# A ScalarE copy of a transposed bf16 tile, with its operands named as fp32

## The chip, the core and the metric

One core of a Trainium2 chip runs one launch of a hand-scheduled kernel. The metric is the device time of a launch in microseconds (us). The core has five engines that run their own instruction streams in order and meet at semaphores: TensorE (PE in the profile; its weight loads are PEld), VectorE (DVE), ScalarE (ACT), GpSimd (POOL) and SyncE (SP), which issues most DMAs.

## What is computed

A transformer block in which attention and a SwiGLU feed-forward stand side by side, forward and backward. Sequence S = 2048, width D = 448, 16 heads of 28, hidden width F = 1792, all operands bf16:

```python
def _fwd_reference(A_x, A_wqkv, A_wo, B_x, B_w_gate, B_w_up, B_w_down):
    x = A_x
    xn = _layernorm(x, axis=-1)
    return x + _A_ref(xn, A_wqkv, A_wo) + _B_ref(xn, B_w_gate, B_w_up, B_w_down)
...
    _out, _vjp = jax.vjp(_f, A_x, A_wqkv, A_wo, B_w_gate, B_w_up, B_w_down)
    _grads = _vjp(grad_out)
```

`_A_ref` is softmax attention over 16 heads, `_B_ref` is (silu(x w_gate) * (x w_up)) w_down. The outputs are the block's output and the gradients of x, wqkv, wo, w_gate, w_up and w_down.

## The kernel before

The launch has three stages. Up to about 626 us the forward attention runs (64 slots of four heads for each of four groups of heads), with the feed-forward and the weight gradients as fillers on TensorE. From there to about 1393 us the attention's backward pass runs; this is the stage the change touches. The rest is the tail, which ends the gradient of x.

The backward stage walks 512 steps (`steps`, L807): group g of four heads, pair of heads hp, key chunk kc of 512, query chunk qc of 512, query tile qi of 128. Four steps, one of each qi, are a block, so there are 128 blocks. At step k the main loop (L1337) issues:

- `row(k)` (L826): four TensorE matmuls of 32x128 by 32x512 in four row groups of the array: two scores of step k into `sb` tiles (L834), two products dP of step k - 1 into `db` tiles (L842).
- `ew(k)` (L854): two ScalarE exps, 128x512 fp32 in PSUM to bf16 `e_sb` (L858), and two VectorE products of step k - 1, `db` times `e_sb` into bf16 `ds_sb` (L864). For the query tiles 0, 1 and 2 of a block, SyncE then issues a DMA that transposes `ds_sb` into `dsT` (L851).
- `kv(k')` (L926): the matmuls that add a step's part of dk and dv into the one `acc` tile (L937, L941). After the last step of a key chunk, every 16 steps, ScalarE copies `acc` into `dkv` (L947).
- where k % 4 is 0, `tr_unit(b)` (L914): the fourth ds tile of block b (in the last block the third too) is not transposed by DMA but by TensorE: eight 128x128 transposes (L919) into one bf16 PSUM tile of 128x1024 that is taken from the `db` tiles, and ScalarE copies it into `dsT` (L924). In the last block the third tile's copy is VectorE's (L922).
- where k % 4 is 1, `dq_unit(b)` (L958): sixteen matmuls of the transposed ds against k (L968) into a `genb` tile, which ScalarE scales into `dq_acc` or `dq_st` (L972, L981); GpSimd then adds `dq_st` to `dq_acc` (L983, L985). In the last group VectorE takes the last of these (L977).
- between these, fillers (`fill_open`, `fill_step`, L1233 to L1251) that use TensorE for other work and one `genb` tile at a time: late weight gradients (`late_dw`, L903), the block's output y (`y_unit`, L1093, evacuated by VectorE at L1098 or L1101), the feed-forward's part of dx (`dx_unit`, L1149; for the first third of F, `fq == 0`, ScalarE evacuates it at L1155, later VectorE adds it at L1157), the attention's part (`dc_unit`, L1196, VectorE at L1200), transposes of dk, dv and dq (`dsp_unit`, `dsq_unit`, L1021, L1002, VectorE at L1024, L1005) and the gradient of wqkv (`dwq_unit`, L1034, VectorE at L1041 to L1044).

The order on every engine is that of these calls: the kernel is recorded with a manual schedule (L132). PSUM is shared out by pools: three `sb` tiles, three `db` tiles (which the transposes share with `row`), one `acc` and one `genb`. A matmul into a tile waits until the tile's last reader is done: for `sb` an exp, for `db` a VectorE product or the copy of L924, for `genb` its evacuation.

The tile that the copy reads and the part of `dsT` that it writes are both 128 partitions of 1024 bf16 elements that lie next to each other, 2048 bytes a partition.

Of the kernel before, what the change touches and what calls it, by code (L numbers as in the profile page):

```python
# [11 lines left out]
FP32 = mybir.dt.float32  # L12
# [93 lines left out]
def kernel(  # L106
# [23 lines left out]
    PE, DVE, ACTE, POOL, SP = nc.tensor, nc.vector, nc.scalar, nc.gpsimd, nc.sync  # L130
# [539 lines left out]
    for t in range(4):  # L670
        run(T_unit(xnT, xn_t, t, t % 2 == 0, ps_s if t < 2 else None))
    DVE.tensor_reduce(out=r_ones[:],
                      in_=ident_f[:].rearrange("p (a b) -> p a b", b=HP)[:, :, 28:30],
# [240 lines left out]
    def tr_unit(b):  # L914
        for qi in (3,) if b < NB // 4 - 1 else (2, 3):
            ds = dss.pop(4 * b + qi)
            ps = ps_b.tile([P, 8, P], BF16, name="db", bufs=3)
            for c in range(8):
                PE.transpose(ps[:, c, :], ds[:, c // 4, (c % 4) * P:(c % 4 + 1) * P], ident_bf[:])  # L919
            o = dsT[b][:, qi].rearrange("p j kt s -> p (j kt) s")  # L920
            if qi == 2:
                DVE.tensor_copy(out=o, in_=ps[:])  # L922
            else:
                ACTE.copy(out=o, in_=ps[:])  # L924

    def kv(k):  # L926
        g, hp, kc, qc, qi = steps[k]
# [409 lines left out]
    for k in range(NB + 12):  # L1337
# [21 lines left out]
        if m == 0:  # L1359
            b = (k - 8) // 4  # L1360
            if 9 <= k < NB and cur is None:
                fill_open(600)
            fill_step(R0)
            if 0 <= b < NB // 4:
                tr_unit(b)
            fill_step(BIG)
        elif m == 1:
            b = (k - 13) // 4
            if 0 <= b < NB // 4:
                dq_unit(b)  # L1370
            if k > NB and k < NB + 8:
                while stream:
                    for _ in stream.pop(0)[1]():
                        pass
                if k < NB + 4:
                    dx_mm(0)
                else:
                    dx_a(0)
                    dx_mm(2)
        elif m == 2:  # L1380
            if 9 <= k < NB:
                fill_open(BIG)
                fill_step(R2)
        else:
            fill_step(R3)
# [59 lines left out]
```

## Time and profile before

| | |
|---|---|
| median of 3 runs | 1437.01 us (1435.54 to 1440.87) |
| span of the profiled execution | 1438.2 us |
| mean granted TensorE clock | 0.982 of full speed |
| ScalarE busy | 1264.2 us of the span |
| of it exps of the backward stage (L858) | 1024 x 611 ns, 555.0 us |
| of it the copy of L924 | 128 x 1016 ns, 130.0 us |
| of it dq evacuations (L981, L972) | 120, 48.0 us |
| of it dkv (L947) | 32 x 709 ns, 22.7 us |
| of it dxg (L1155) | 16 x 560 ns, 9.0 us |
| VectorE products (L864) | 1024 x 685 ns, 646.5 us |

The profile is one execution. Busy times of operations that overlap in an engine's pipeline are counted once, so a group's busy time is less than its count times the mean of one. An idle time before an instruction is named with what ended it: `[0.20 <-PE db L842]` is 0.20 us of idle that ended when TensorE's instruction of L842, into `db`, was done. TensorE's matmuls are pipelined and their ends are modelled: the start of one against the start of the next says more than the busy share. The granted clock is the share of TensorE's full clock that was allowed.

Busy tenths of the span in 40 slices of 36 us, TensorE, VectorE and ScalarE:

```
PE   5899999989999999989999989999999999999995
DVE  6677757656666676578999989888899999999988
ACT  4799988989889998869999989999989999899974
```

### The profile page before, as it was taken

The numbers are of one execution on the slowest core, as the hardware profiler recorded it, in microseconds if no ns is written. First come the engines' busy times: TensorE is split into PE (matmuls) and PEld (weight loads), VectorE is DVE, ScalarE is ACT, GpSimd is POOL, SyncE is SP. The second block draws the span as 40 slices with busy tenths as digits, with TensorE's granted clock in tenths as the row PEclk, the third lists the DMA queues.
The fourth block names the chain that finished last, engine by engine and source line by source line (L and its number), as shares of the span: only waits on it lengthen the run. The fifth ranks groups of instructions, "written<-read, shape, count | busy, mean of one in ns | idle before, by whom it ended". The sixth has DMA issues, their size and how long they took to land. (4 is left out here: it accounts for less than half of the span.)

```text
span 1438.2 us, 34638 instructions
## 1 busy us (share of the span) xinstructions
PE 1321.2 (92%) x12625; PEld 539.0 (37%) x12686; DVE 1154.8 (80%) x2001; ACT 1264.2 (88%) x2190; POOL 411.8 (29%) x577
## 2 busy tenths in 40 slices
PE   5899999989999999989999989999999999999995
PEld 2333333333333333333343434433443334443333
DVE  6677757656666676578999989888899999999988
ACT  4799988989889998869999989999989999899974
POOL 6574514454434454211121211201111112020005
PEclk9999999999999999989999999999999999999998
DMA  5796957796578676699999999999999999999981
GB/s 154 183 205 160 237 116 169 179 190 157 149 164 191 153 155 153 176 243 233 219 213 227 206 227 173 221 219 223 223 169 200 200 216 218 212 186 207 190 142 60
DMA packets 681116, 270.22 MB, mean 188 GB/s; under 512 B 607338, under 2 KB 655970, under 8 KB 680946
## 3 DMA queue, kind: packets, MB, share of 16 engines
q1 hardware_dynamic: 672498, 254.78, 87.1%
q0 software_dynamic: 7040, 12.93, 4.1%
q8 instruction: 99, 1.62, 0.5%
q14 instruction: 71, 0.58, 0.1%
q10 hardware_dynamic: 1408, 0.30, 0.1%
HBM read 64.37 MB, written 59.62 MB: 86 GB/s over the span
## 5 line engine op out<-in xcount | busy, mean ns | idle before, releaser
L864 DVE TENSOR_TENSOR ds_sb<-db,e_sb 128x512 bf16<-128x512 f32 x1024 | 646.5, 685 | 48.6 <-issue 22.4
L858 ACT ACTIVATE e_sb<-sb 128x512 bf16<-128x512 f32 x1024 | 555.0, 611 | 53.7 <-PE db L842 37.1
L628 ACT ACTIVATE eT<-s_w 128x1024 bf16<-128x1024 f32 x256 | 263.8, 1030 | 47.0 <-PE s_ps L625 43.8
L630 ACT ACTIVATE eT<-s_ps 128x512 bf16<-128x512 f32 x512 | 280.2, 611 | 0.0
L842 PE MATMUL db<-kd,qd 32*128 32x512 bf16 x1024 | 238.0, 385 | 8.6 <-DVE ds_sb L864 7.5
L834 PE MATMUL sb<-kd,qd 32*128 32x512 bf16 x1024 | 210.9, 389 | 5.3 <-DMA qd<-QD_d 3.4
L983 POOL TENSOR_TENSOR dq_acc<-dq_acc,dq_st 128x256 f32<-128x256 f32 x64 | 46.4, 724 | 497.7 <-ACT dq_st L981 497.7
L941 PE MATMUL acc<-ds_sb,qd 128*32 128x512 bf16 x1024 | 161.3, 391 | 0.0
L937 PE MATMUL acc<-e_sb,qd 128*32 128x512 bf16 x1024 | 159.2, 392 | 1.3 <-DVE dw_o L544 1.3
L924 ACT COPY dsT<-db 128x1024 bf16<-128x1024 bf16 x128 | 130.0, 1016 | 18.4 <-PE db L919 17.3
L396 POOL TENSOR_TENSOR nn<-nn,ag 128x512 f32<-128x512 f32 x56 | 71.3, 1274 | 249.7 <-DVE ag L394 241.1
L625 PE MATMUL s_ps<-QQ,KK 32*128 32x512 bf16 x512 | 126.2, 385 | 4.1
L1149 PE MATMUL genb<-wguT,dau_c 128*128 128x448 bf16 x448 | 117.5, 355 | 6.3 <-ACT dq_st L981 3.9
L625 PE MATMUL s_w<-QQ,KK 32*128 32x512 bf16 x512 | 100.2, 387 | 12.8 <-ACT eT L628 9.8
L834 PEld LDWEIGHTS <-qd 32*128 32x128 bf16 x1024 | 48.2, 91 | 146.3 <-issue 136.9
L437 PE MATMUL gen<-xn_t,f_sp 128*128 128x448 bf16 x416 | 91.8, 354 | 2.6 <-DVE nn L411 1.7
L437 PEld LDWEIGHTS <-f_sp 128*128 128x128 bf16 x640 | 55.7, 98 | 76.7 <-issue 31.6
L919 PE MATMUL db<-ident_bf,ds_sb 128*128 128x128 bf16 x1032 | 80.3, 222 | 0.9 <-DVE ds_sb L864 0.9
L968 PE MATMUL genb<-dsT,kd 128*32 128x256 bf16 x2048 | 79.2, 274 | 1.1
L919 PEld LDWEIGHTS <-ds_sb 128*128 128x128 bf16 x1032 | 69.1, 99 | 23.6 <-issue 5.1
L397 POOL TENSOR_TENSOR nn<-nn,tt 128x512 f32<-128x512 f32 x56 | 72.1, 1287 | 4.4
L625 PEld LDWEIGHTS <-KK 32*128 32x128 bf16 x1024 | 29.1, 91 | 115.3 <-issue 112.5
(179 smaller groups left out, 1951.7 us busy)
## 6 DMA issues: line engine op xcount, KB each, us to landing
F_d<-hda SPq DMA_DIRECT2D x56, 384.0 KB
dau_c<-F_d SPq DMA_DIRECT2D x24, 512.0 KB
qd<-QD_d SPq DMA_DIRECT2D x16, 512.0 KB
kd<-KD_d SPq DMA_DIRECT2D x16, 384.0 KB
dsT<-ds_sb SPq DMA_TRANSPOSE x383
h_c<-F_d SPq DMA_DIRECT2D x8, 512.0 KB
wT_d<-wT_f SPq DMA_DIRECT2D x14, 256.0 KB
KD_d<-qk_sp SPq DMA_DIRECT2D x7, 512.0 KB
```

The lines of the kernel that those rows point to most:

```text
L437: PE.matmul(ps[:, :D], lhsT=fsp[fc][:, t // 4, w, t % 4, :], rhs=rhs[:, t, :], start=(t == 0), stop=(t == NT - 1))
L625: PE.matmul(sp4[hh], lhsT=KK[g][r:r + HP, kt * P:(kt + 1) * P], rhs=QQ[g][r:r + HP, qsl], start=True, stop=True, tile_position=(r, 0))
L628: ACTE.activation(out=e2[0][:], in_=wide[:], func=ACT.Exp, scale=SCALE)
L630: ACTE.activation(out=e2[1][:, j], in_=sp4[2 + j], func=ACT.Exp, scale=SCALE)
L834: PE.matmul(s_ps[:], lhsT=qside[g, qc][r:r + HP, 0, qi * P:(qi + 1) * P], rhs=kside[g, kc][r:r + HP, 0, :], start=True, stop=True, tile_po ...
L842: PE.matmul(d_ps[:], lhsT=qside[g, qc][r:r + HP, 1, qi * P:(qi + 1) * P], rhs=kside[g, kc][r:r + HP, 1, :], start=True, stop=True, tile_po ...
L858: ACTE.activation(out=est[k][:, j], in_=sps.pop((k, j))[:], func=ACT.Exp, scale=SCALE)
L864: DVE.tensor_tensor(out=ds[:, j], in0=dps.pop((k - 1, j))[:], in1=est[k - 1][:, j], op=ALU.mult)
L919: PE.transpose(ps[:, c, :], ds[:, c // 4, (c % 4) * P:(c % 4 + 1) * P], ident_bf[:])
L924: ACTE.copy(out=o, in_=ps[:])
L937: PE.matmul(a[r:r + HP, :], lhsT=sp4[:, 1, r:r + HP], rhs=e[:, j, :], start=first, stop=last, tile_position=(0, r), skip_group_check=True)
L941: PE.matmul(a[r:r + HP, :], lhsT=sp4[:, 0, r:r + HP], rhs=ds[:, j, :], start=first, stop=last, tile_position=(0, r), skip_group_check=True)
```

## The change

```diff
@@ -921,7 +921,7 @@
             if qi == 2:
                 DVE.tensor_copy(out=o, in_=ps[:])
             else:
-                ACTE.copy(out=o, in_=ps[:])
+                ACTE.copy(out=o.bitcast(FP32), in_=ps[:].bitcast(FP32))
```

ScalarE's copy reads the same 2048 bytes of a partition and writes the same 2048 bytes, but both operands are named as 512 fp32 elements where they were 1024 bf16 elements. Two neighbouring bf16 values travel as the two halves of one fp32 word. Nothing else in the program's text changes: the transposes still write bf16, and the dq product still reads bf16. VectorE's one copy at L922 stays as it was.

## The prediction

> **What bounds the kernel now.** I read the page first for the engines and the costliest groups, then the busy time of single blocks (a block is the stretch from one L924 copy to the next, 128 in all), then the timelines of three kinds of block.
>
> ```profile
> PE 1321.2 (92%) x12625; PEld 539.0 (37%) x12686; DVE 1154.8 (80%) x2001; ACT 1264.2 (88%) x2190; POOL 411.8 (29%) x577
> L858 ACT ACTIVATE e_sb<-sb 128x512 bf16<-128x512 f32 x1024 | 555.0, 611 | 53.7 <-PE db L842 37.1
> L924 ACT COPY dsT<-db 128x1024 bf16<-128x1024 bf16 x128 | 130.0, 1016 | 18.4 <-PE db L919 17.3
> ```
>
> The copy is 130.0 us of ScalarE, all after 633 us. Now the busy times (length, PE, PEld, DVE, ACT, POOL) of an ordinary block, one that ends a dkv, one that evacuates dxg on ScalarE, and the whole steady stage:
>
> ```profile
> 1137.24:1142.87 5.63, 5.58 (x65) 2.18 (x64) 5.47 (x10) 5.35 (x11) 0.00 (x0) 1.00 1.16 153
> 1130.93:1137.24 6.31, 5.75 (x65) 2.36 (x64) 5.59 (x10) 5.79 (x12) 0.00 (x0) 1.00 1.01 193
> 948.53:954.44 5.91, 5.82 (x68) 2.37 (x67) 5.04 (x9) 5.71 (x13) 0.00 (x0) 1.00 1.07 236
> 660.00:1390.00 730.00, 695.33 (x7993) 292.26 (x7992) 669.48 (x1122) 673.74 (x1252) 107.34 (x165) 0.99 1.10 206
> ```
>
> In the ordinary block VectorE idles 0.16 us and ScalarE 0.28; in the dxg block ScalarE idles 0.20 and VectorE 0.87. So the engine with least slack changes from block to block, and each kind must be costed alone. An ordinary block (from 1095.95) on VectorE, ScalarE and TensorE:
>
> ```profile
> 1096.84 1.28 DVE L864 TENSOR_TENSOR ds_sb<-db,e_sb 128x512 bf16<-128x512 f32 x2
> 1098.28 3.74 DVE L864 TENSOR_TENSOR ds_sb<-db,e_sb 128x512 bf16<-128x512 f32 x6 [0.16 <-issue]
> ...
> 1100.61 1.09 ACT L858 ACTIVATE e_sb<-sb 128x512 bf16<-128x512 f32 x2 [0.20 <-PE db L842]
> ...
> 1096.02 0.80 PE L842 MATMUL db<-kd,qd 32*128 32x512 bf16 x2
> 1097.19 0.61 PE L968 MATMUL genb<-dsT,kd 128*32 128x256 bf16 x16
> 1097.74 0.39 PE L842 MATMUL db<-kd,qd 32*128 32x512 bf16 x2
> ```
>
> Its loop has no ScalarE in it. L842's 0.80 us is two matmuls of 0.37 to 0.39 with a stall between: the second waits for a db tile that VectorE frees at about 0.45 us into the block. From there TensorE issues without a gap (acc, the dq product, the next row at 1097.74), the row ends at 1098.13, VectorE starts at 1098.28 and runs six products, 3.74 us, whose end frees the db tile of the next block. 0.45 to 2.33 us on TensorE and 3.74 us on VectorE make 5.62 of 5.63. ScalarE waits 0.20 us for TensorE inside that time: it is not late.
>
> **The change, part by part.**
>
> *The price of one copy.* No row shows a 128x512 f32 to f32 copy from PSUM. Nearest are L1155, 128x448 f32 from f32, 560 ns, and the bf16 copies of 512 and 1024 elements (L340 587, L924 1016). The bf16 pair gives (1016-587)/512 = 0.838 ns an element; 560 + 64 x 0.838 = 614. Bounds: 587 (the bf16 copy of 512) and 640 (L386, 512 f32 to f32). I take 614, since L1155 has both operand types. Each copy ends 402 ns earlier (376 to 429), and the next ScalarE operation, which now starts 0.89 us after the copy starts, may start at 0.49. Over 128 copies ScalarE loses 51.5 us of work. What reaches the end is counted by kind of block:
>
> *Ordinary blocks and those that evacuate y (L1101):* nothing. The exp after the copy comes 0.40 earlier or, in the y blocks, still waits for a row that TensorE is late with (it starts 1.04 to 1.07 after the copy began, the copy having ended at 1.02); the next row is set by the loop above. The cover is ScalarE's own wait, which grows from 0.28 to 0.68. The same holds for the blocks of dwq (exp at 1.17 or later). If the cover were gone, 0.40 each would show.
>
> *The 16 blocks with L1155* (925 to 1025 us). There the dxg evacuation sits behind the copy, and TensorE's dq product, which reuses the genb tile, waits for it:
>
> ```profile
> 949.42 0.56 ACT L1155 COPY dxg<-genb 128x448 f32<-128x448 f32 x1
> 949.55 0.38 PE L937 MATMUL acc<-e_sb,qd 128*32 128x512 bf16 x2
> 950.03 0.62 PE L968 MATMUL genb<-dsT,kd 128*32 128x256 bf16 x16
> ```
>
> From that L937 to L968 are 0.48 us; in the ordinary block it is 0.21 (1096.98 to 1097.19). The evacuation can begin 0.33 earlier (genb's last matmul ends 0.51 into the block), so the whole stall goes: 0.26. What is late next is VectorE's loop of the ordinary block, at 5.63 to 5.65, just where 5.91 - 0.26 lands. 12 plain blocks x 0.26 = 3.1. In the four that also end a dkv (6.75 long, 8.07 once) ScalarE's chain copy, dxg, two exps, dkv, dq holds TensorE, which waits for dq; it moves by 0.33: 4 x 0.33 = 1.3.
>
> *Blocks that end a dkv.* ScalarE runs without a gap from the copy to the dq evacuation, and TensorE waits for it:
>
> ```profile
> 1132.79 0.72 ACT L947 ACTIVATE dkv<-acc,cols 128x512 bf16<-128x512 f32 x1
> 1132.17 0.38 PE L941 MATMUL acc<-ds_sb,qd 128*32 128x512 bf16 x2
> 1133.84 0.35 PE L1149 MATMUL genb<-wguT,dau_c 128*128 128x448 bf16 x1 [0.52 <-ACT dq_acc L972]
> ```
>
> dkv can't start before acc is done, 1132.55 to 1132.56, plus 0.06 to signal (so much later dkv starts in the one block where it waits for acc alone, at 840.18): 0.18 earlier than 1132.79, not 0.40. VectorE follows, having 0.37 and 0.26 us of waits in that block. Eleven blocks are of this form: 11 x 0.18 = 2.0. Two early ones and one before a dsp transpose give 0.45 together. In the other 14 of the 32 dkv blocks the exp is held by TensorE, or VectorE has no slack: nothing.
>
> *Six blocks after a dsp unit* (5.41 us, as 1114.27 to 1119.68) run on ScalarE and VectorE both; VectorE's wait of 0.12 goes: 0.7.
>
> *What the change adds.* As built, all engines keep their order, but the db tiles go round otherwise in four of the first eight blocks: the second db matmul of the row after the transposes gets the very tile that the copy frees, and waits for ScalarE where it waited for VectorE. Behind it on TensorE stand the acc matmuls, dq and the next row, for which VectorE waits. The copy lets go 0.66 after its start; that matmul starts 0.55 after it in three of the blocks and 0.18 in the first. Loss: 3 x 0.11 + 0.48 = 0.8; bounds 0 (a later wait covers it) and 1.5 (it comes again). The tail gains nothing: its last copies stand beside VectorE's dx work.
>
> Sum: 3.1 + 1.3 + 2.0 + 0.45 + 0.7 - 0.8 = 6.8 us, against the profiled execution's span of 1438.2, which is 1.2 above the median of the runs. Taken off the median: 1430.2. The price of the copy hardly matters: at 640 ns it still gives 376 ns, more than any block uses.
>
> The stage's occupancy is 673.74 us for ScalarE, 669.48 for VectorE. [...]
>
> **The rivals.**
>
> *VectorE takes over as the bound, and its waits go too.* If ScalarE's earlier exps also dissolved VectorE's 0.16 us in 36 ordinary blocks and 0.30 in 11 y blocks, 5.8 + 3.3 us would come on top: 1421.1. For it: VectorE is within 5 us of ScalarE over the stage. Against: the releaser of those waits is TensorE's row, which waits for VectorE.
>
> *Nothing arrives.* The blocks that gain are given back at the transposes by DMA or at the next dkv, or the copy in fp32 is no shorter: 1437. For it: three waits of VectorE for a ds tile that its DMA still reads, 3.1 us together. Against: 560 ns for 448 fp32 elements.
>
> *Slower: TensorE's clock drops more often.* Blocks with dsp transposes come with and without a drop: 7.80 us at a mean granted clock of 0.87 (716.17) against 7.04 at 1.00 (811.95), and 7.64 against 6.88. One drop costs 0.76. A shift of all phases can move drops; it decides from nine more on (6.8/0.76). With 20 more: 1437 - 6.8 + 15.2 = 1445. Against: the stage shows four or so in 730 us, and TensorE's idle time shrinks. [...]
>
> **How the numbers follow.** The forecast has 0.60, VectorE's bound 0.18, nothing 0.14, slower 0.08. About 0.5%, 7.2 us, is what a measurement can tell from no change: faster means below 1429.8. The forecast's own range is 1426 to 1434 (6.8 with a few drops or DMA waits either way, and the bounds above) and lies astride that line, about half on each side: 0.30 + 0.18 = 0.48 faster; 0.30 + 0.14 = 0.44 same; 0.08 slower. The range takes in the VectorE case and the case of nothing: 1420 to 1437.
>
> **What would show it.** L924 at about 614 ns x128, the ordinary block still at 5.63 with ScalarE idle about 0.68 in it, the dxg block at 5.65, the dkv block at 6.13, and L968 no longer held by L1155. An ordinary block below 5.55, or L924 above 700 ns, would make the prediction wrong; so would dxg blocks that stay at 5.91.

## The result, and the profile after

The changed kernel took 1433.64 us (median of 10 runs, 1429.33 to 1436.28), the kernel before 1440.36 us on the same chip (10 runs, 1435.54 to 1443.47). The ratio is 0.9962, 95% interval 0.9946 to 0.9977: 0.2% to 0.5% faster. The profiled execution of the changed kernel has a span of 1427.5 us, against 1438.2. Of those 10.7 us, 4.7 lie before the first L924 copy (at 628.5 us, before at 633.2), in a part that the change doesn't touch; from the first copy to the last it is 763.3 us before and 756.7 after, 6.6 us less; the tail is 0.7 longer.

Page of the changed kernel, first its engines, then two of the costliest groups (busy us, mean ns, idle time before):

```profile
PE 1318.6 (92%) x12625; PEld 540.2 (38%) x12686; DVE 1152.4 (81%) x2001; ACT 1219.0 (85%) x2190; POOL 411.0 (29%) x577
L858 ACT ACTIVATE e_sb<-sb 128x512 bf16<-128x512 f32 x1024 | 552.5, 601 | 75.8 <-PE db L842 58.0
L924 ACT COPY dsT<-db 128x512 f32<-128x512 f32 x128 | 75.4, 589 | 17.5 <-PE db L919 16.4
```

The copy does what the change says: 1016 ns have become 589. ScalarE lost 54.6 us of copying (130.0 less 75.4); the stage became 6.6 us shorter, an eighth of that. Part of the rest stands in the second line: before its exps ScalarE now waits 75.8 us, 22 more than before, mostly for TensorE. Before the dq evacuations (L981, L972) it waits 15 us more. And its whole busy time fell by 45.2 us only (1264.2 to 1219.0), as its operations overlap less: their single times add to 1473 us before and 1404 after, so that some 209 us overlapped before and 185 after.

The same kinds of block as in the prediction, now in the changed kernel (stretch, length; busy time of TensorE, weight loads, VectorE, ScalarE, GpSimd; clock, DMA share, GB/s). In this order: dxg on ScalarE, dxg with a dkv, after a dsp unit, a dkv, ordinary:

```profile
944.29:949.92 5.63, 5.63 (x68) 2.42 (x67) 5.04 (x9) 5.38 (x13) 0.00 (x0) 1.00 1.11 236
955.55:961.91 6.36, 5.79 (x68) 2.50 (x67) 5.15 (x9) 5.84 (x13) 0.73 (x1) 1.00 1.14 252
1106.08:1111.38 5.30, 5.30 (x65) 2.22 (x64) 5.25 (x10) 5.00 (x11) 0.73 (x1) 1.00 1.21 151
1122.64:1128.81 6.17, 5.83 (x65) 2.36 (x64) 5.49 (x10) 5.46 (x12) 0.00 (x0) 1.00 1.09 223
1128.81:1134.44 5.63, 5.58 (x65) 2.18 (x64) 5.47 (x10) 5.03 (x11) 0.00 (x0) 1.00 1.16 166
```

The ordinary block is 5.63 us as before; ScalarE's idle time in it grew from 0.28 to 0.60 and nothing else moved. The dxg block fell from 5.91 to the same 5.63, with TensorE now busy from end to end; with a dkv it fell from 6.75 to 6.36, the dkv block from 6.31 to 6.17, the block after a dsp unit from 5.41 to 5.30.

The dxg block of the changed kernel, from its timeline (start us, us, engine):

```profile
944.83 0.53 ACT L1155 COPY dxg<-genb 128x448 f32<-128x448 f32 x1
945.31 0.38 PE L937 MATMUL acc<-e_sb,qd 128*32 128x512 bf16 x2
945.53 0.61 PE L968 MATMUL genb<-dsT,kd 128*32 128x256 bf16 x16
```

From L937 to L968 are now 0.22 us, where 0.48 were. The evacuation starts 0.54 us into the block, not 0.89, and L968 has stopped waiting for it.

### The profile page after: what moved, and what is told of

It reads as the page before. It is cut to its first block, busy times and chain, and to the rows that moved or that the text cites. A ratio compares the mean times of both kernels' runs of the same rounds, so it can differ in the third digit from the quotient of the medians.

```text
span 1427.5 us, 34631 instructions
## 1 busy us (share of the span) xinstructions
PE 1318.6 (92%) x12625; PEld 540.2 (38%) x12686; DVE 1152.4 (81%) x2001; ACT 1219.0 (85%) x2190; POOL 411.0 (29%) x577
## 5 line engine op out<-in xcount | busy, mean ns | idle before, releaser
L858 ACT ACTIVATE e_sb<-sb 128x512 bf16<-128x512 f32 x1024 | 552.5, 601 | 75.8 <-PE db L842 58.0
L937 PE MATMUL acc<-e_sb,qd 128*32 128x512 bf16 x1024 | 158.3, 390 | 1.3 <-DVE dw_o L544 1.3
L625 PE MATMUL s_w<-QQ,KK 32*128 32x512 bf16 x512 | 100.0, 386 | 13.2 <-ACT eT L628 10.4
L924 ACT COPY dsT<-db 128x512 f32<-128x512 f32 x128 | 75.4, 589 | 17.5 <-PE db L919 16.4
L968 PE MATMUL genb<-dsT,kd 128*32 128x256 bf16 x2048 | 80.0, 277 | 0.0
```

What stands on the lines that cost most here:

```text
L625: PE.matmul(sp4[hh], lhsT=KK[g][r:r + HP, kt * P:(kt + 1) * P], rhs=QQ[g][r:r + HP, qsl], start=True, stop=True, tile_position=(r, 0))
L858: ACTE.activation(out=est[k][:, j], in_=sps.pop((k, j))[:], func=ACT.Exp, scale=SCALE)
L937: PE.matmul(a[r:r + HP, :], lhsT=sp4[:, 1, r:r + HP], rhs=e[:, j, :], start=first, stop=last, tile_position=(0, r), skip_group_check=True)
```

## The experiments

All kernels were profiled, and those compared in time ran 6 or 12 times, with the kernel before beside them on the same chip. Single runs of one kernel spread over 10 us and more, and go with the TensorE clock that they were granted: over 175 runs, with one straight line for all and a constant for each kernel on each chip, a clock lower by 0.01 goes with 9.4 us more, and 2.2 us of scatter remain, where 3.4 are left without the clock. Where "at equal clock" is said, it is the difference to the kernel before from that fit, with its 95% bounds; what a change does to the clock itself is not in it. Block lengths need none of this: undisturbed, one block of one kernel repeats from run to run to 0.01 us, seldom 0.02.

**The same kernel again, and the copy split by blocks.** Four kernels on one chip:

> The changed kernel a second time. Theory (the gain sits in blocks where ScalarE's copy stands before something that TensorE waits for): the same 5 to 7 us below the kernel before, and the same lengths of single blocks to 0.02 us (ordinary 5.63, dxg 5.63, dkv 6.17). Rival (the gain is a lucky placing of clock drops and DMA waits): the block lengths stay as they are, but the time moves by several us, as other blocks carry the drops.

> The copy named fp32 only in the 17 blocks from 48 to 64, where L1155 evacuates dxg on ScalarE; bf16 in the other 111. Theory: 12 x 0.28 + 4 x 0.38 = 4.9 us less than before, about 1435.5 where the kernel before has 1440.4, and dkv blocks elsewhere at 6.31. Rival (every copy pays its share): 17/128 of the gain, 0.8 us.

> The complement: bf16 in blocks 48 to 64, fp32 in the other 111. Theory: dxg blocks stay at 5.91 and 6.75; 11 dkv blocks x 0.135 + 6 blocks after a dsp unit x 0.12 + 0.4 = 2.6 us less than before, less up to 0.8 for the first eight blocks: 1.8 to 2.6. Rival (every copy pays its share): 111/128 of the gain, 5 to 6 us.

> fp32 from block 8 on; the first eight keep bf16 copies, and with them, if the tiles go round as before, the waits of the second db matmul for VectorE. Theory: at or up to 0.8 us below the changed kernel, and in blocks 5 to 7 the second db matmul starts some 0.55 after the copy, not 0.64. Rival (the early waits are hidden): the same time as the changed kernel.

```diff
+            elif 48 <= b < 65:
+                ACTE.copy(out=o.bitcast(FP32), in_=ps[:].bitcast(FP32))
             else:
                 ACTE.copy(out=o, in_=ps[:])
```

(the second, against the kernel before; the third has `not 48 <= b < 65`, the fourth `b >= 8`.) Measured, with the kernel before at 1438.62 (35 runs); lengths of blocks 52 (dxg), 82 (dkv) and 83 (ordinary):

| copy in fp32 | median, us | ratio, 95% | at equal clock, us | dxg | dkv | ordinary |
|---|---|---|---|---|---|---|
| everywhere, again | 1436.57 | 0.9985 (0.9962 to 1.0008) | -5.2 ± 1.5 | 5.63 | 6.18 | 5.63 |
| blocks 48 to 64 | 1436.70 | 0.9998 (0.9974 to 1.0022) | -3.0 ± 1.5 | 5.63 | 6.31 | 5.63 |
| all but 48 to 64 | 1439.54 | 1.0004 (0.9987 to 1.0022) | -1.3 ± 1.5 | 5.91 | 6.18 | 5.63 |
| from block 8 on | 1433.80 | 0.9968 (0.9947 to 0.9989) | -5.7 ± 1.4 | 5.63 | 6.18 | 5.63 |

The dxg block in the busy times of the second kernel:

```profile
949.46:955.09 5.63, 5.63 (x68) 2.41 (x67) 5.03 (x9) 5.38 (x12) 0.00 (x0) 1.00 1.09 218
```

and in those of the third:

```profile
950.26:956.17 5.91, 5.82 (x68) 2.37 (x67) 5.03 (x9) 5.71 (x12) 0.00 (x0) 1.00 1.09 224
```

Lengths follow the naming block by block, to 0.01 us. Seventeen copies of 128 carry 3.0 us of gain and the other 111 1.3, which add to 4.3 of the 5.2. The 3.0 ± 1.5 falls short of the 4.9 that were expected and that the lengths of these blocks show; why, the record doesn't tell. The rival by which each copy pays its share, 0.8 and 5 to 6, is out. The medians alone would not have told this: at 12 runs each their intervals hold no change in three of the four. The rival of lucky drops is out for the block lengths, but by the fit drops are what makes the median of the repeat so much nearer to that of the kernel before. Its mean clock was 0.9773 beside 0.9799; in the runs of the first result it was 0.9799. All four kernels here had a lower clock than the kernel before (0.9773 to 0.9790); the kernels with moved evacuations below had a slightly higher one (0.9798 to 0.9803 beside 0.9790 and 0.9791). Whether the change brings some more drops stays open.

The early wait is there and of the predicted size: in blocks 5 to 7 the second db matmul starts 0.64 us after the copy in the changed kernel and 0.55 in the fourth one, 0.09 each. In the time it can't be seen. The first block took between 6.28 and 10.28 us over these and the next profiles, half-clock stretches (a granted clock of 0.50 from 632 to 636 us in the kernel before) and loads that come late included.

**What of the copy pays: its time on ScalarE, or that it lets go sooner?**

> The fp32 copy, with a second ScalarE copy of 288 bf16 elements from SBUF to a scratch tile behind it, some 0.4 us: ScalarE has about the time of the kernel before, but frees the db tile and finishes dsT early. Theory (what pays is that the operations behind the copy come earlier): all of the gain goes, dxg blocks back at 5.9, dkv blocks at 6.31, ordinary at 5.63. Rival (what pays is the early release of db or dsT): dxg 5.63 and dkv 6.17 stay.

> The bf16 copy with the same extra 0.4 us behind it. Theory: the ordinary block has 0.25 to 0.28 us of cover on ScalarE, so it grows by what is over that, 0.1 to 0.2, from 5.63 to 5.75 or 5.85; dxg blocks, with 0.0 to 0.05 of it, by nearly all, from 5.91 to 6.25 or 6.3. Rival (the ordinary block has no ScalarE in its loop at all): it stays at 5.63. Rival (VectorE and ScalarE wait for each other in every block): it grows by the whole 0.4.

```diff
+                ACTE.copy(out=scr[:], in_=xn_t[:, :288])
```

(behind the fp32 copy in the first, behind the bf16 copy in the second.) One run each, 1438.44 and 1457.18 us, the kernel before 1440.05. The extra copy is 0.44 us, and the next operation starts 0.34 after it. Dxg, dkv and ordinary block, of the fp32 copy with the extra, then of the bf16 copy with it:

```profile
950.39:956.20 5.81, 5.81 (x68) 2.37 (x67) 5.04 (x9) 5.61 (x14) 0.00 (x0) 1.00 1.02 217
1130.22:1136.43 6.21, 5.75 (x65) 2.35 (x64) 5.57 (x10) 5.68 (x13) 0.00 (x0) 1.00 1.03 197
1136.43:1142.06 5.63, 5.58 (x65) 2.17 (x64) 5.47 (x10) 5.34 (x12) 0.00 (x0) 1.00 1.04 207
```

```profile
954.20:960.44 6.24, 5.82 (x68) 2.38 (x67) 5.04 (x9) 6.03 (x14) 0.00 (x0) 1.00 1.04 213
1143.28:1149.91 6.63, 5.77 (x65) 2.34 (x64) 5.58 (x10) 6.10 (x14) 0.00 (x0) 1.00 1.05 204
1149.90:1155.65 5.75, 5.70 (x65) 2.34 (x64) 5.52 (x10) 5.56 (x12) 0.00 (x0) 1.00 1.03 179
```

In the first kernel the dxg evacuation starts 0.80 us into its block (951.19 less 950.39):

```profile
951.19 0.56 ACT L1157 COPY dxg<-genb 128x448 f32<-128x448 f32 x1
```

It is the line called L1155 elsewhere, two lines down in this file. So a start at 0.89, 0.80, 0.54 goes with lengths of 5.91, 5.81, 5.63: by 0.09 the block follows in full, and of the next 0.26 it takes 0.18, as then the ordinary loop is the longest. With the db tile let go at the changed kernel's early time, two thirds of the dxg gain were gone all the same (0.18 of 0.28): it is ScalarE's queue that pays. The dkv block says the same: the dkv starts 1.76 us into it, 0.10 earlier than in the kernel before, and the block is 0.10 shorter, 6.21. All of the gain was expected to go, with 5.9 and 6.31; the extra was 0.09 too short for that (the price of an extra ScalarE operation is its start-to-start time, not its 0.44). In the second kernel the ordinary block grew by 0.12, not by 0 and not by the whole extra. That is its cover measured: the dxg block, which has none, grew by 0.33, so that 0.21 was hidden, somewhat less than the idle time of 0.25 to 0.28. The y blocks (5.85, 5.88) moved by 0.03 at most even then.

**Two blocks relieved in another way.**

> The kernel before, with its bf16 copy, and the 16 dxg evacuations of L1155 on VectorE. Theory: these blocks become ordinary ones, 5.63, and those with dkv 6.31, so that two thirds of the change's gain comes without touching the copy. Rival (the copy itself holds these blocks): they stay near 5.9.

> The kernel before with L1157's addition on VectorE cut to 224 of 448 columns (the other half of the dxg sum is left out), which takes some 0.25 us of VectorE out of the ordinary blocks of the dx stage. Theory: the loop of the ordinary block is TensorE from the second db matmul to the row, then six products; L1157 stands beside the TensorE half, so its time turns into idle time of VectorE (0.16 to about 0.4) and the block stays at 5.63. Rival (VectorE is the bound by its load): the block falls to about 5.4.

```diff
-            ACTE.copy(out=o, in_=ps[:, :D])
+            DVE.tensor_copy(out=o, in_=ps[:, :D])
```

```diff
-            DVE.tensor_tensor(out=o, in0=ps[:, :D], in1=o, op=ALU.add)
+            DVE.tensor_tensor(out=o[:, :224], in0=ps[:, :224], in1=o[:, :224], op=ALU.add)
```

With the evacuation on VectorE (0.625 us there) and the bf16 copy, the dxg block; and the ordinary block of the kernel before with half the addition (0.386 us, where 0.62 were), which leaves out the other half of that part of dx:

```profile
953.09:958.78 5.69, 5.69 (x68) 2.34 (x67) 5.54 (x10) 5.43 (x12) 0.00 (x0) 1.00 1.11 232
```

```profile
1136.51:1142.14 5.63, 5.58 (x65) 2.18 (x64) 5.24 (x10) 5.34 (x11) 0.00 (x0) 1.00 1.02 212
```

The first falls from 5.91 to 5.69 with the old copy: the two ScalarE operations in a row were the cause. Not quite to 5.63, as expected; the block with a dkv came to 6.30. The whole run was no faster, 1446.09 in its single run beside 1440.05, with a clock of 0.973, blocks 5 to 7 at 22.5 us together (18.1 in the kernel before, but 22.5 also in the kernel with fp32 in blocks 48 to 64) and block 64 at 8.37 with TensorE waiting 2.6 for a q load; a single run tells something by its blocks alone. In the second, 0.23 us of VectorE's work went (5.47 to 5.24) and the ordinary block kept its 5.63: VectorE's load doesn't set it, though VectorE is 97% busy there. In blocks like 88, of 5.69, where VectorE runs without a gap from the addition to the last product, the same edit took off 0.06. The totals, 1438.78 beside 1440.05, are single runs and say nothing either way.

**Using the time that ScalarE has gained.** The blocks with dsp transposes are left at 6.5 and more. In the changed kernel, in the first block of each of ten pairs, TensorE waits for an evacuation of VectorE that itself stands behind a product (timeline, block 67):

```profile
1038.18 0.68 DVE L1005 COPY dsp<-genb 128x1024 bf16<-128x1024 bf16 x1
...
1038.91 0.55 PE L1002 MATMUL genb<-ident_bf,dqT 128*128 128x128 bf16 x7 [0.82 <-DVE dsp L1005]
```

> The changed kernel with the 20 dsp evacuations of the stage (L1005, L1024, 0.69 us of VectorE each) moved to ScalarE and named fp32, 0.59 us each; the four in the tail, on ScalarE already, are named fp32 too. They fall in ten pairs of blocks: in the first (6.52 to 6.68 undisturbed) TensorE waits 0.82 us for the VectorE evacuation, which is queued behind a product; in the second (5.30) VectorE idles 0.05. Theory (ScalarE's freed time is worth something only where work of the bound engine is put there): on ScalarE the first ends some 0.35 sooner and VectorE loses 0.69 in each, so the first block falls to 6.2 or 6.3, the second by 0 to 0.2: 3 to 5 us below the changed kernel. Rival (TensorE's transposes and rows set these blocks): nothing moves. Rival on the other side (ScalarE's exps come late behind the evacuation): the second block grows by some 0.3, which eats the gain.

> The same move made in the kernel before: 20 evacuations on ScalarE in bf16, some 1.01 us each, and the ds copy in bf16. Theory: ScalarE idles 0.12 to 0.19 in the second block of a pair and has no room for 1.01, so that block grows by 0.5 or more, 5 us or more slower than before over ten pairs. Rival (ScalarE has room anyway): as fast as the move in fp32 made the changed kernel.

> The changed kernel with the same 20 evacuations left on VectorE but named fp32 (the four in the tail, on ScalarE, as well). If naming halves the elements for VectorE as it did for ScalarE, 0.69 us falls to some 0.4 and the pairs lose some of it. By the nearest row, L1155 moved to VectorE (448 fp32 elements, 0.625 us), 512 take about 0.69: nothing for VectorE, and the time of the changed kernel less up to 1 us in the tail.

```diff
-        (ACTE.copy if tag == "rest" else DVE.tensor_copy)(out=dsp[g][:, 8 * t8:8 * t8 + 8, kind, :], in_=ps[:])
+        ACTE.copy(out=dsp[g][:, 8 * t8:8 * t8 + 8, kind, :].bitcast(FP32), in_=ps[:].bitcast(FP32))
```

(and L1005 in the same way; the second has the bf16 operands of the kernel before, the third keeps the engine and takes the fp32 operands.) The kernel before had 1441.35 (29 runs).

| 20 evacuations | median, us | ratio, 95% | at equal clock, us | blocks 67 + 68 |
|---|---|---|---|---|
| ScalarE, fp32 | 1434.43 | 0.9959 (0.9937 to 0.9981) | -5.8 ± 1.5 | 6.05 + 5.63 |
| ScalarE, bf16, ds copy bf16 | 1446.61 | 1.0034 (1.0016 to 1.0052) | +6.1 ± 1.5 | 6.48 + 6.49 |
| VectorE, fp32 | 1435.68 | 0.9958 (0.9938 to 0.9978) | -4.3 ± 1.5 | 6.52 + 5.40 |

In the changed kernel the pair is 6.52 + 5.40. The move in bf16 makes the kernel before slower, so the room on ScalarE is the change's doing. In fp32 the first block falls by 0.47 and the second grows by 0.23, since there the evacuation stands between the copy and the exp: theory and the rival on the other side were both right, one in each half. Against the changed kernel's ratio of 0.9962, moving all twenty brought nothing that can be measured, where 3 to 5 us were expected. On VectorE the name is worth nothing (group of costliest instructions, third kernel, 686 ns before):

```profile
L1024 DVE COPY dsp<-genb 128x512 f32<-128x512 f32 x14 | 9.6, 685 | 1.3 <-PE genb L1021 1.3
```

So the last kernel moves only the first of each pair:

> Of each pair of dsp evacuations only the first goes to ScalarE, the second stays on VectorE; all 24 are named fp32. Theory (work moved to ScalarE pays where VectorE is queued and ScalarE has idle time in that very block, and costs where it stands between the copy and the next exp): the first block of a pair falls by some 0.5, as when both were moved (67: 6.52 to 6.05; 99: 6.58 to 6.25), the second stays at 5.30 where it had grown to 5.53: 4 to 5 us below the changed kernel over ten pairs, and some 1 us more from the tail, about 10 us or 0.7 per cent below the kernel before. Rival (the gain of the first block is only moved to the second): the pair's sum stays at that of the changed kernel, 11.8 to 12.0.

```diff
+        (ACTE.copy if tag == "rest" or t8 == 0 else DVE.tensor_copy)(out=dsp[g][:, 8 * t8:8 * t8 + 8, kind, :].bitcast(FP32), in_=ps[:].bitcast(FP32))
```

It took 1431.37 us (6 runs) beside 1440.13 (11 runs), 0.9926 (0.9903 to 0.9949), 8.0 ± 2.2 us less at equal clock. Against the kernel before it is a clear gain; it did not run beside the changed kernel, and their intervals touch. Blocks 67 and 68, then block 64 and what TensorE waited for in it:

```profile
1041.56:1047.61 6.05, 5.64 (x76) 2.62 (x76) 5.87 (x10) 5.52 (x12) 0.00 (x0) 1.00 1.08 242
1047.61:1053.00 5.39, 5.39 (x69) 2.45 (x69) 5.26 (x9) 5.06 (x10) 0.00 (x0) 1.00 1.12 165
```

```profile
1021.31:1029.75 8.44, 6.50 (x67) 2.33 (x65) 5.83 (x10) 5.48 (x12) 3.22 (x5) 1.00 1.19 245
```

```profile
1028.37 0.39 PE L834 MATMUL sb<-kd,qd 32*128 32x512 bf16 x2 [1.46 <-DMA qd<-QD_d]
```

The pair is 11.44, 0.48 less than in the changed kernel. Over the ten pairs it is 3.6 us less than undisturbed ones of the changed kernel, a little short of the 4 to 5 expected: eight fall by 0.24 to 0.64, one by 0.06, and blocks 99 and 100 grow by 0.49. In this profile most of that is given back: block 64, 5.63 in the changed kernel, takes 8.44 in this profile, TensorE waiting 1.46 us of that for a q load. The kernel that moved all twenty had the same wait (1.52), and so had the one that named them fp32 on VectorE (2.18) and the one with dxg on VectorE: the move is not what brings it. In the profiles of the kernel before and of the changed one that load came in time. It is not only that a faster kernel gets there sooner: the changed kernel reached the block 387.5 us after its first copy and did not wait, the one with dxg on VectorE after 389.7 and did; the one with fp32 from block 8 on after 385.4 and did not, the last one after 385.6 and did. What decides it stays open. The tail, from the last copy to the end, is 41.0 us here and in the other two kernels that name its evacuations fp32 on a ds copy in fp32, 41.9 and 42.3 in the two profiles of the changed kernel.

## Why the prediction was right

- **The price of the copy.** Predicted 614 ns with bounds of 587 and 640; it is 589. The price hardly mattered, as said: the operation behind the copy could start 0.42 us earlier, and no block used more than 0.39.
- **Ordinary, y and dwq blocks: nothing.** Right, to 0.03 us, but for blocks 11 and 12, 120 and 121, where a wait of VectorE comes later: the first of each two is 0.33 shorter, the second 0.12 and 0.39 longer. With fp32 from block 8 on they are as before, so this goes back to the copies of the first eight blocks. The cover named, ScalarE's own wait, grew to 0.60 where 0.68 was predicted, and the extra copy used it up as it should. The loop of TensorE and VectorE in the ordinary block held against halving an operation of VectorE outside it; that a shorter operation inside it would shorten the block was not tried.
- **Dxg blocks: 12 x 0.26 and 4 x 0.33.** Measured 12 x 0.28 and 4 x 0.38, 4.9 us for 4.4. The named next bound is where they stopped: 5.63, predicted 5.65. L968's wait was 0.26 of the 0.28.
- **Dkv blocks: 11 x 0.18.** Measured 11 x 0.135. The dkv does start 0.18 earlier (1.68 us into the block, not 1.86), for the reason given: it then waits for acc. What the sum left out is the next step behind it: the second db matmul of the following row then waits for VectorE, which gives 0.04 to 0.05 back.
- **After a dsp unit: 6 x 0.12; two early blocks and one before a dsp transpose: 0.45.** Measured 0.12 each (0.11 to 0.13), and in two blocks more, 15 and 95, where the profile before had a drop of the clock; 0.16 in one early block, 0.20 before the dsp transpose (block 78, 6.88 to 6.68); the other early one can't be told from late loads.
- **The early wait: -0.8.** In blocks 5 to 7 it is there with 0.09 each for 0.11. In the first block the matmul starts 0.64 after the copy for the predicted 0.66, but with the bf16 copy it started at 0.18 in the kernel before and at 0.55 in the fourth kernel, and the loads and clock drops of the first eight blocks move by more than the whole term: no run shows its 0.48.
- **The sum.** 6.8 us were predicted. The two medians differ by 6.7, the copy-to-copy time of the two profiles by 6.6, and at equal clock the repeat gave 5.2 ± 1.5. The forecast of 1430.2 took the gain off a median of 3 runs, 1437.0; ten runs beside the changed kernel put that at 1440.4, and so the changed kernel at 1433.6. (The prediction also set a span, 1438.2, beside a median of times; a run's time is some 1.8 us more than its span.) The terms as the blocks show them, the wait of blocks 5 to 7 taken off, add to 7.4. So the kinds of block were right, while it is partly luck that two of the totals come within 0.2 of 6.8: between the two profiles of the first result the first eight blocks grew by 3.8 us and the others lost 10.4, drops and late loads included, and from copy to copy the second and third kernel, with a part of the gain each, took 764.8 and 764.7, longer than the kernel before. That less than 7.4 shows at equal clock stays open.
- **The rivals.** VectorE's waits did not dissolve: 0.16 in the ordinary block as before. Something did arrive. The drops of the clock didn't undo the gain, but they are what hides it: 0.01 of clock goes with 9.4 us, more than the change. The prediction's price of a drop, 0.76, is too low: it counted the first block of a pair alone, and the drop runs on into the second. The pair took 1.1 more in the kernel before (7.80 + 5.78 against 7.04 + 5.42) and 1.4 in the changed one (7.62 + 6.08 against 7.04 + 5.30 in the repeat), so that five or six more drops would have undone the gain, not nine. The stretches before the drops were not idle ones: TensorE was busy for 0.33 to 0.71 of them (last section). In the profiles the pairs show three drops before, three in the changed kernel and one in the repeat.
- **The stage's occupancy.** Of the two engines that the prediction compares, 673.74 us for ScalarE and 669.48 for VectorE, the first lost 54.6 us of copying and the time fell by an eighth of that; halving an operation of the second (0.62 to 0.386 us) gave nothing in the ordinary block either. Here occupancy showed neither what the ordinary block waits for nor the size of the gain.

## What to carry to other kernels

Cost a faster instruction by the kinds of stretch it stands in: in each, find who waits next for what comes behind it, and stop at the loop that is then the longest. ScalarE was 95% busy in the ordinary block (5.35 of 5.63 us) and a shorter copy gave nothing there; its freed time paid here only where another engine's late work was put into it: the first of each pair of evacuations paid (0.47 us in blocks 67 and 68), the second cost half as much as the first had gained (0.23). Where the clock moves single runs by more than the gain, compare lengths of like stretches in the profiles, which repeated here to a hundredth of a microsecond, and take the medians for the sum only.

## What the runs showed of the hardware

- Naming bf16 pairs as fp32 takes a ScalarE copy of 128x1024 bf16 from PSUM from 1016 to 589 ns (1.72 times faster), in the evacuations with a strided target too (means of 593 and 621 ns against 1019 and 1056). The same on VectorE changed nothing: 686 and 685 ns. In these copies ScalarE's time went with the number of elements (587 ns for 512 bf16 at L340, 589 for 512 fp32, 1016 for 1024 bf16), VectorE's did not (686 for 1024 bf16, 685 for 512 fp32). The naming was tried on copies out of PSUM only.
- Operations that follow each other on ScalarE overlap: the next one starts 0.47 to 0.54 us after a copy of 0.59, so the gain of a shorter one is better read from starts than from durations. L1155 itself became shorter, 533 ns for 560, without being touched.
- The granted clock, recorded in steps of 0.001, goes with 60% of the variance between runs of one kernel: 9.4 us for 0.01.
- The granted clock dropped to 0.50 for 3.41 us at a time, or multiples of it. From block 8 to block 124 the fourteen profiles show 26 drops, and each began behind a stretch of 3.41 us in which TensorE was busy for 0.33 to 0.71 of the time; of 2803 such stretches without a drop behind them 18 were as low. So waits that leave TensorE busy for two thirds of a stretch came before a drop; what decides whether a wait of a dsp pair is followed by one was not shown. One such stretch of the kernel before and the one behind it (here the busy times are TensorE's first, and the clock stands behind GpSimd's):

```profile
718.54:721.95 3.41, 2.31 (x24) 1.01 (x21) 3.21 (x6) 3.41 (x8) 2.68 (x5) 1.00 0.92 199
721.95:725.36 3.41, 3.19 (x32) 2.03 (x35) 2.65 (x6) 1.66 (x3) 0.54 (x2) 0.50 1.32 175
```
